# A parallel attention and FFN block: a tile of x loaded ahead, the layer norm's root taken off ScalarE, statistics held back, FFN steps moved up

## The chip, the cores and the metric

One core of a Trainium2 chip. The metric is the device time of one execution in microseconds (us), the median over several runs. The engines go by short names: PE is TensorE (matmuls), DVE VectorE, ACT ScalarE. PSUM is where the matmuls leave their results; a buffer there must be read out before it is used again.

## The reference, cut to what matters

S = 2048 rows, D = 512 columns, F = 1792, H = 32 heads of 16. The inputs are bf16.

```python
xn = _layernorm(x)                       # (x - mean) / sqrt(var + 1e-5), per row
# attention without softmax
q, k, v = split(xn @ wqkv)               # D -> 3 D
phi = lambda t: where(t > 0, t + 1, exp(t)) + 1e-6
kv  = einsum("bhsd,bhse->bhde", phi(k), v);  z = sum over s of phi(k)
o   = (phi(q) @ kv) / (phi(q) . z + 1e-6)
# the FFN, on the same xn
f   = (silu(xn @ w_gate) * (xn @ w_up)) @ w_down
out = x + o @ wo + f
```

`kv` and `z` need every row of k and v, so the attention can't begin before all 16 tiles of 128 rows are through the layer norm and the k and v projections. The FFN of a block of 512 rows needs only that block's `xn`, so its matmuls serve as filling.

## The kernel before: the parts that matter

Loads, all from one queue, in this order (block b of x is 512 rows, 512 KB):

```python
    for b in range(NB):                                   # 4 blocks
        nc.sync.dma_start(out=xb[:], in_=x2d[b * TB : (b + 1) * TB, :]...)
        if b == 0:
            nc.sync.dma_start(out=wqkv_sb[:], in_=A_wqkv...)   # 1.5 MB, q, k and v columns
    nc.sync.dma_start(out=wg_sb[:], in_=B_w_gate...)      # 1.75 MB
    nc.sync.dma_start(out=wu_sb[:], in_=B_w_up...)        # 1.75 MB
    # ... wo, w_down
```

Statistics of a block: for four tiles, then the reciprocal of a square root, improved by one Newton step:

```python
    def ln_stats_block(bb):
        for tt in range(TPB):                             # 4 tiles
            nc.vector.bn_stats(out=stats[:], in_=xbb[:, tt, :])
            nc.vector.bn_aggr(out=mv_blk[:, tt, :], in_=stats[:])
        nc.scalar.activation(out=std_blk[:], in_=mv_blk[:, :, 1], func=ACTF.Sqrt, bias=eps_ln[:], scale=1.0)
        nc.vector.reciprocal(out=rstd_blk[:], in_=std_blk[:])
        # ... vpe, and a Newton step of three operations
```

The loop. What a tile passes through, and on which engine:

```python
    stats_blk[0] = ln_stats_block(0)
    for b in range(NB):
        for tt in range(TPB):
            if tt == 1 and b + 1 < NB:
                stats_blk[b + 1] = ln_stats_block(b + 1)
            nc.vector.tensor_scalar(out=xn[:], ...)                # DVE
            # 4 transposes xn -> tp (PSUM)                         # PE
            nc.scalar.copy(out=xnT[...], in_=tp[:])                # ACT
            # 4 matmuls k_ps, 4 matmuls v_ps; both share 2 PSUM buffers ("mm")
            nc.scalar.activation(out=ek[:], in_=k_ps[:], func=ACTF.Exp)   # ACT
            # ek = min(ek, 1) + eps; pk_all = max(k_ps + 1, ek)    # DVE, frees k_ps
            nc.scalar.copy(out=v_aug[...], in_=v_ps[:]...)         # ACT, frees v_ps
            if b >= 1:
                ffn_issue(1 if b < 3 else 2, max_block=b - 1)      # low priority
        for g in range(NG):
            # 4 matmuls q_ps; eq = Exp on ACT; pqT on DVE
            ...
```

The program gives the order of priority; a scheduler makes each engine's order of it, and FFN steps have low priority, so their matmuls land where others would wait.

## Time and profile before

| | before |
|---|---|
| median, us | 241.65 (240.89 to 241.94, 16 runs) |
| profiled span, us | 239.9 |
| TensorE (PE) busy | 222.4 (93%) |
| mean granted clock | 0.993 |
| first transpose / first k matmul, us | 8.92 / 10.21 |
| loads of tables on ScalarE (ACT) | 8 |

The kernel is bound by PE, except in its first 25 us. From the view of PE's waits of the kernel before, these lines matter here, by the line that waits and the one that it waits for; the columns at the end are us in total, how often, and the longest. Left out are 2.1 us before x has landed and two short waits of 0.3 and 0.2:

```profile
PE tp L259 <- DVE xn L249: 6.5, 1, 6.5
PE k_ps L266 <- ACT xnT L260: 2.3, 2, 2.0
...
PE v_ps L266 <- DVE pk_all L283: 1.0, 2, 0.5
PE k_ps L266 <- ACT v_aug L291: 0.4, 2, 0.2
```

The first line is the start, the second the pause at 16 to 18 us which a swap of tables on ACT makes, the last two are PSUM buffers that come free late.

### The profile page before, as it was taken

The page shows a single profiled execution, that of the slowest core. Times are in us where ns is not written, and L with a number is a line of the kernel's source. Part 1 is how long each engine was busy: PE and PEld are TensorE (multiplying, and loading weights), DVE is VectorE, ACT ScalarE, POOL GpSimd, SP SyncE. Part 2 cuts the span into 40 slices and gives each one's busy share as a digit, 9 for nine tenths or more (in the row PEclk, how much of TensorE's full clock was granted, in tenths as well). Part 3 has the DMA queues.
Part 4 walks back from the last instruction along what each step waited for, and adds up shares of the span by engine and source line. Part 5 has one row for each costly group of instructions (what it writes and reads, how often), then busy time and mean ns, then how long its engine had stood idle before and what let it go on. Part 6 is the DMA issues. An engine that isn't in the chain of part 4 may idle for free.

```text
span 239.9 us, 3281 instructions
## 1 busy us (share of the span) xinstructions
PE 222.4 (93%) x1226; PEld 107.2 (45%) x1250; DVE 140.8 (59%) x324; ACT 120.6 (50%) x204; POOL 1.4 (1%) x9
## 2 busy tenths in 40 slices
PE   0469999999999999999999999999999999999994
PEld 0224455444444465444445544444554444454441
DVE  3898697686595799652129765212986521386121
ACT  2489997666656647764006566500566640056000
POOL 2000000000000000000000000000000000000000
PEclk9997999999999999999999999999999999999999
DMA  6999700000000000000000000000000000100001
GB/s 245 364 405 379 229 0 0 1 3 0 0 0 0 3 0 4 0 0 0 25 22 23 3 22 0 0 22 25 22 23 3 0 0 22 44 25 0 23 25 44
DMA packets 8352, 12.01 MB, mean 50 GB/s; under 512 B 400, under 2 KB 6800, under 8 KB 8336
## 3 DMA queue, kind: packets, MB, share of 16 engines
q1 hardware_dynamic: 8336, 11.80, 13.9%
q8 instruction: 10, 0.16, 0.3%
q14 instruction: 6, 0.05, 0.1%
HBM read 9.70 MB, written 2.10 MB: 49 GB/s over the span
## 4 chain that ended last, share of the span: by engine, by line
PE 85%; DVE 6%; ACT 6%; DMA 1%; issue 1%
PE o_ps L213 20%; PE g_ps L176 19%; PE u_ps L176 19%; PE o_ps L205 6%; PE v_ps L266 5%; PE k_ps L266 5%; PE q_ps L302 5%; PE otp L388 2%; ACT xnT L260 2%; PE num_ps L363 2%; DMA xb<-in_A_x_dram 1%; DVE stats L144 1%; PE tp L259 1%; DVE pqT L319 1%; ACT eq L310 1%
## 5 line engine op out<-in xcount | busy, mean ns | idle before, releaser
L186 ACT ACTIVATE uh<-u_ps 128x512 bf16<-128x512 f32 x56 | 33.7, 603 | 53.9 <-DVE hTf L197 42.5
L176 PE MATMUL g_ps<-xnT,wg_sb 128*128 128x512 bf16 x214 | 59.0, 380 | 0.7 <-issue 0.2
L176 PE MATMUL u_ps<-xnT,wu_sb 128*128 128x512 bf16 x219 | 58.5, 379 | 0.2
L213 PE MATMUL o_ps<-wd_sb,hTf 128*128 128x512 bf16 x219 | 51.2, 379 | 0.3
L188 DVE SCALAR_TENSOR_TENSOR wst<-th,g_ps 128x512 bf16<-128x512 bf16 x56 | 38.1, 681 | 20.0 <-ACT th L184 19.9
L184 ACT ACTIVATE th<-g_ps 128x512 bf16<-128x512 f32 x56 | 33.7, 602 | 17.7 <-PE g_ps L176 17.4
L221 DVE TENSOR_TENSOR o_t<-o_ps,xb 128x512 bf16<-128x512 f32 x16 | 11.1, 691 | 50.9 <-PE o_ps L213 50.8
L213 PEld LDWEIGHTS <-hTf 128*128 128x128 bf16 x224 | 21.5, 98 | 24.6
L176 PEld LDWEIGHTS <-wu_sb 128*128 128x128 bf16 x224 | 21.6, 98 | 23.9 <-issue 0.4
L176 PEld LDWEIGHTS <-wg_sb 128*128 128x128 bf16 x224 | 21.3, 99 | 22.1 <-issue 0.6
L197 DVE TENSOR_TENSOR hTf<-wst,uh 128x512 bf16<-128x512 bf16 x56 | 23.3, 421 | 5.9 <-ACT uh L186 5.7
L266 PEld LDWEIGHTS <-xnT 128*128 128x128 bf16 x128 | 12.7, 100 | 21.2 <-issue 6.2
L266 PE MATMUL k_ps<-wqkv_sb,xnT 128*128 128x512 bf16 x64 | 17.3, 394 | 2.7 <-ACT xnT L260 2.3
L266 PE MATMUL v_ps<-wqkv_sb,xnT 128*128 128x512 bf16 x63 | 17.3, 399 | 1.0 <-DVE pk_all L283 1.0
L205 PE MATMUL o_ps<-wo_sb,oT 128*128 128x512 bf16 x62 | 16.3, 379 | 0.1
L302 PE MATMUL q_ps<-xnT,wqkv_sb 128*128 128x512 bf16 x63 | 15.7, 378 | 0.1
L274 ACT ACTIVATE ek<-k_ps 128x512 f32<-128x512 f32 x16 | 9.7, 608 | 6.4 <-PE k_ps L266 5.9
L310 ACT ACTIVATE eq<-q_ps 128x512 f32<-128x512 f32 x16 | 9.8, 610 | 6.2 <-PE q_ps L302 5.1
L144 DVE BATCH_NORM_STATS2 stats<-xb 128x6 f32<-128x512 bf16 x16 | 10.5, 677 | 3.4 <-DMA xb<-in_A_x_dram 3.4
L259 PE MATMUL tp<-ident,xn 128*128 128x128 bf16 x64 | 6.1, 242 | 6.5 <-DVE xn L249 6.5
L380 DVE TENSOR_TENSOR o_sb<-num_ps,rden 128x512 bf16<-128x512 f32 x16 | 11.0, 688 | 1.9 <-PE num_ps L363 1.4
L291 ACT CAST v_aug<-v_ps 128x512 bf16<-128x512 f32 x16 | 9.6, 598 | 4.3 <-PE v_ps L266 4.0
(49 smaller groups left out, 148.2 us busy)
## 6 DMA issues: line engine op xcount, KB each, us to landing
xb<-in_A_x_dram SPq DMA_DIRECT2D x4, 512.0 KB, 8.5
out_dram<-o_t SPq DMA_DIRECT2D x16, 128.0 KB, 1.7
wg_sb<-in_B_w_gate_dram SPq DMA_DIRECT2D x1, 1792.0 KB, 12.6
wu_sb<-in_B_w_up_dram SPq DMA_DIRECT2D x1, 1792.0 KB, 15.6
wd_sb<-in_B_w_down_dram SPq DMA_DIRECT2D x1, 1792.0 KB, 19.4
wqkv_sb<-in_A_wqkv_dram SPq DMA_DIRECT2D x1, 1536.0 KB, 7.1
wo_sb<-in_A_wo_dram SPq DMA_DIRECT2D x1, 512.0 KB, 15.7
```

What stands on the lines that cost most here:

```text
L144: nc.vector.bn_stats(out=stats[:], in_=xbb[:, tt, :])
L176: nc.tensor.matmul(dst[:], lhsT=w_sb[:, c, f * P : (f + 1) * P], rhs=xnT[:, c, b * TB : (b + 1) * TB], start=(c == 0), stop=(c == DC - 1),)
L184: nc.scalar.activation(out=th[:], in_=g_ps[:], func=ACTF.Tanh, scale=0.5)
L186: nc.scalar.activation(out=uh[:], in_=u_ps[:], func=ACTF.Copy, scale=0.5)
L188: nc.vector.scalar_tensor_tensor(out=wst[:], in0=th[:], scalar=1.0, in1=g_ps[:], op0=ALU.add, op1=ALU.mult,)
L197: nc.vector.tensor_tensor(out=hTf[:], in0=wst[:], in1=uh[:], op=ALU.mult)
L205: nc.tensor.matmul(o_ps[:], lhsT=oT[:, c, t * P : (t + 1) * P], rhs=wo_sb[:, c, :], start=(c == 0), stop=False,)
L213: nc.tensor.matmul(o_ps[:], lhsT=hT_tiles[(b, f)][:, tt * P : (tt + 1) * P], rhs=wd_sb[:, f, :], start=False, stop=(f == FC - 1),)
L221: nc.vector.tensor_tensor(out=o_t[:], in0=o_ps[:], in1=xb_tiles[b][:, tt, :], op=ALU.add)
L266: nc.tensor.matmul(dst[:], lhsT=xnT[:, c, t * P : (t + 1) * P], rhs=wqkv_sb[:, c, (j + 1) * D : (j + 2) * D], start=(c == 0), stop=(c == D ...
L302: nc.tensor.matmul(q_ps[:], lhsT=wqkv_sb[:, c, g * P : (g + 1) * P], rhs=xnT[:, c, b * TB : (b + 1) * TB], start=(c == 0), stop=(c == DC - 1),
L310: nc.scalar.activation(out=eq[:], in_=q_ps[:], func=ACTF.Exp)
```

## The change

Its intent: begin the matmuls earlier, and take the swaps of tables out of the way of the first blocks. Four parts:

1. *Loads.* The first tile of x (128 KB) alone, then the other three; the k and v columns of `wqkv` in two halves of rows, then the q columns; the first 512 columns of `w_gate` and `w_up` right after block 1 of x, the rest after all of x.
2. *Root.* The first tile's statistics by themselves; 1/sqrt from the bits (a constant minus half the bits) and two Newton steps, nine small operations on VectorE (DVE), no `Sqrt` on ACT.
3. *Gates.* The statistics of tiles 1 to 3 are issued only after a copy that follows the first `xn`; those of block b + 1 only after block 0's third `xn`, and after block b's tiles in program order.
4. *FFN.* Two FFN steps of a block may follow directly on its q.

```diff
         xb = res.tile([P, TPB, D], BF16, name=f"xb{b}")
+        if b == 0:
+            nc.sync.dma_start(out=xb[:, 0, :], in_=x2d[0:P, :])
+            nc.sync.dma_start(out=xb[:, 1:TPB, :], in_=x2d[P:TB, :]...)
+            for half in range(2):                       # k and v columns
+                nc.sync.dma_start(out=wqkv_sb[:, 2 * half : 2 * half + 2, D:QKV], ...)
+            nc.sync.dma_start(out=wqkv_sb[:, :, 0:D], ...)
         ...
+        if b == 1:
+            FA = 512
+            for dst, src in ((wg_sb, B_w_gate), (wu_sb, B_w_up)):
+                nc.sync.dma_start(out=dst[:, :, 0:FA], in_=src[:, 0:FA]...)
+    for dst, src in ((wg_sb, B_w_gate), (wu_sb, B_w_up)):
+        nc.sync.dma_start(out=dst[:, :, FA:F], in_=src[:, FA:F]...)
 ...
-        nc.scalar.activation(out=std_blk[:], in_=mv_blk[:, :, 1], func=ACTF.Sqrt, ...)
-        nc.vector.reciprocal(out=rstd_blk[:], in_=std_blk[:])
-        # one Newton step
+        # ve = var + eps; ih = bits(ve) >> 1; bits(rstd) = 1597463007 - ih
+        for _ in range(2):
+            # Newton step: three operations on DVE
 ...
-    stats_blk[0] = ln_stats_block(0)
+    stats_blk[0] = ln_stats_block(0, 0, 1)
 ...
-            if tt == 1 and b + 1 < NB:
-                stats_blk[b + 1] = ln_stats_block(b + 1)
+            if b == 0 and tt == 1:
+                with tc.issue_after(hm_copy.ins):
+                    ln_stats_block(0, 1, TPB, tiles=stats_blk[0])
 ...
+            if b == 0 and tt == 2:
+                xn_gate = xn_ins
 ...
+        if b + 1 < NB:
+            with tc.issue_after(xn_gate.ins):
+                stats_blk[b + 1] = ln_stats_block(b + 1)
 ...  # q
+        ffn_issue(2, max_block=b)
```

More of the change, by code (lines that the diff above doesn't have):

```diff
@@ L12 @@
 F32 = mybir.dt.float32
+I32 = mybir.dt.int32
 @with_exitstack
@@ L73 @@
         xb = res.tile([P, TPB, D], BF16, name=f"xb{b}")
+        if b == 0:
+            nc.sync.dma_start(out=xb[:, 0, :], in_=x2d[0:P, :])
+            nc.sync.dma_start(
+                out=xb[:, 1:TPB, :],
+                in_=x2d[P:TB, :].rearrange("(t p) d -> p t d", p=P),
+            )
+            wqkv_sb = res.tile([P, DC, QKV], BF16, name="wqkv_sb")
+            for half in range(2):
+                nc.sync.dma_start(
+                    out=wqkv_sb[:, 2 * half : 2 * half + 2, D:QKV],
+                    in_=A_wqkv[half * 2 * P : (half + 1) * 2 * P, D:QKV].rearrange(
+                        "(c p) f -> p c f", p=P
+                    ),
+                )
+            nc.sync.dma_start(
+                out=wqkv_sb[:, :, 0:D], in_=A_wqkv[:, 0:D].rearrange("(c p) f -> p c f", p=P)
+            )
+        else:
+            nc.sync.dma_start(
+                out=xb[:],
+                in_=x2d[b * TB : (b + 1) * TB, :].rearrange("(t p) d -> p t d", p=P),
+            )
+        xb_tiles.append(xb)
+        if b == 1:
+            FA = 512
+            wg_sb = res.tile([P, DC, F], BF16, name="wg_sb")
+            wu_sb = res.tile([P, DC, F], BF16, name="wu_sb")
+            for dst, src in ((wg_sb, B_w_gate), (wu_sb, B_w_up)):
+                nc.sync.dma_start(
+                    out=dst[:, :, 0:FA], in_=src[:, 0:FA].rearrange("(c p) f -> p c f", p=P)
+                )
+    for dst, src in ((wg_sb, B_w_gate), (wu_sb, B_w_up)):
         nc.sync.dma_start(
-            out=xb[:],
-            in_=x2d[b * TB : (b + 1) * TB, :].rearrange("(t p) d -> p t d", p=P),
-        )
-        xb_tiles.append(xb)
-        if b == 0:
-            wqkv_sb = res.tile([P, DC, QKV], BF16, name="wqkv_sb")
-            nc.sync.dma_start(
-                out=wqkv_sb[:], in_=A_wqkv.rearrange("(c p) f -> p c f", p=P)
-            )
-    wg_sb = res.tile([P, DC, F], BF16, name="wg_sb")
-    nc.sync.dma_start(out=wg_sb[:], in_=B_w_gate.rearrange("(c p) f -> p c f", p=P))
-    wu_sb = res.tile([P, DC, F], BF16, name="wu_sb")
-    nc.sync.dma_start(out=wu_sb[:], in_=B_w_up.rearrange("(c p) f -> p c f", p=P))
+            out=dst[:, :, FA:F], in_=src[:, FA:F].rearrange("(c p) f -> p c f", p=P)
+        )
     wo_sb = res.tile([P, DC, D], BF16, name="wo_sb")
@@ L126 @@
     nc.tensor.matmul(hm_ps[:], lhsT=e8[:], rhs=ident[:HG, :HG], start=True, stop=True)
-    nc.vector.tensor_copy(out=hm8[:], in_=hm_ps[:])
+    hm_copy = nc.vector.tensor_copy(out=hm8[:], in_=hm_ps[:])
     xnT = res.tile([P, DC, S], BF16, name="xnT")
@@ L137, with ln_stats_block @@
     nc.vector.memset(v_aug[:, :, :, P : P + 1], 1.0)
-    def ln_stats_block(bb):
+    def ln_stats_block(bb, t0=0, t1=TPB, tiles=None):
         xbb = xb_tiles[bb]
-        mv_blk = pb.tile([P, TPB, nc.vector.BN_AGGR_DIM], F32, name="mv_blk")
-        for tt in range(TPB):
+        if tiles is None:
+            mv_blk = pb.tile([P, TPB, nc.vector.BN_AGGR_DIM], F32, name="mv_blk")
+            rstd_blk = pb.tile([P, TPB], F32, name="rstd_blk")
+        else:
+            mv_blk, rstd_blk = tiles
+        n = t1 - t0
+        for tt in range(t0, t1):
             stats = pb.tile([P, nc.vector.BN_STATS_DIM], F32, name="stats")
@@ L145, in ln_stats_block @@
             nc.vector.bn_aggr(out=mv_blk[:, tt, :], in_=stats[:])
-        std_blk = pb.tile([P, TPB], F32, name="std_blk")
-        nc.scalar.activation(
-            out=std_blk[:], in_=mv_blk[:, :, 1], func=ACTF.Sqrt, bias=eps_ln[:], scale=1.0
-        )
-        rstd_blk = pb.tile([P, TPB], F32, name="rstd_blk")
-        nc.vector.reciprocal(out=rstd_blk[:], in_=std_blk[:])
-        vpe = pb.tile([P, TPB], F32, name="vpe")
+        ve = pb.tile([P, TPB], F32, name="ve")
+        nc.vector.tensor_scalar(
+            out=ve[:, t0:t1], in0=mv_blk[:, t0:t1, 1], scalar1=EPS_LN, scalar2=None, op0=ALU.add
+        )
+        ih = pb.tile([P, TPB], I32, name="ih")
         nc.vector.tensor_scalar(
-            out=vpe[:], in0=mv_blk[:, :, 1], scalar1=EPS_LN, scalar2=-0.5, op0=ALU.add, op1=ALU.mult
+            out=ih[:, t0:t1], in0=ve[:, t0:t1].bitcast(I32), scalar1=1, scalar2=None,
+            op0=ALU.logical_shift_right,
+        )
+        nc.vector.tensor_scalar(
+            out=rstd_blk[:, t0:t1].bitcast(I32), in0=ih[:, t0:t1], scalar1=-1.0, scalar2=1597463007.0,
+            op0=ALU.mult, op1=ALU.add,
         )
         nrt = pb.tile([P, TPB], F32, name="nrt")
-        nc.vector.tensor_tensor(out=nrt[:], in0=rstd_blk[:], in1=rstd_blk[:], op=ALU.mult)
-        nc.vector.tensor_tensor(out=nrt[:], in0=nrt[:], in1=vpe[:], op=ALU.mult)
-        nc.vector.scalar_tensor_tensor(
-            out=rstd_blk[:],
-            in0=nrt[:],
-            scalar=1.5,
-            in1=rstd_blk[:],
-            op0=ALU.add,
-            op1=ALU.mult,
-        )
+        for _ in range(2):
+            nc.vector.tensor_tensor(out=nrt[:, t0:t1], in0=rstd_blk[:, t0:t1], in1=rstd_blk[:, t0:t1], op=ALU.mult)
+            nc.vector.scalar_tensor_tensor(
+                out=nrt[:, t0:t1], in0=nrt[:, t0:t1], scalar=-0.5, in1=ve[:, t0:t1], op0=ALU.mult, op1=ALU.mult
+            )
+            nc.vector.scalar_tensor_tensor(
+                out=rstd_blk[:, t0:t1], in0=nrt[:, t0:t1], scalar=1.5, in1=rstd_blk[:, t0:t1],
+                op0=ALU.add, op1=ALU.mult,
+            )
         return mv_blk, rstd_blk
@@ L248 @@
             xn = pb.tile([P, D], BF16, name="xn")
-            nc.vector.tensor_scalar(
+            xn_ins = nc.vector.tensor_scalar(
                 out=xn[:],
```

## The prediction

> **What bounds the kernel now.** I read the page's busy shares first, then its slices.
>
> ```profile
> PE 222.4 (93%) x1226; PEld 107.2 (45%) x1250; DVE 140.8 (59%) x324; ACT 120.6 (50%) x204; POOL 1.4 (1%) x9
> ...
> PE   0469999999999999999999999999999999999994
> ...
> PEclk9997999999999999999999999999999999999999
> ```
>
> TensorE (PE) is busy from slice 4 on and slack only in slices 1 to 3 and the last: the kernel is TensorE-bound except in its first 25 us or so. The second line to read is the granted clock: slice 4 (18 to 24 us) falls to 0.7. The chain of waits confirms it: 85% of the span lies on PE.
>
> How much time is loose? Steady matmuls of 512 columns start 0.216 us apart (the chain view has 14 of L213 in 3.02 us). Transposes and other 128-column matmuls start about 0.056 apart. The program has 928 of the first kind (200.3 us), 256 of the second (14.3 us) and 64 tiny ones (1.6 us): 216.2 us of work. The first transpose starts at 8.92 and the last matmul ends at 236.5, 227.6 us later. So some 11.4 us are lost between them, 8.9 before them, and 3.4 after. By the same count of what was issued, 8.92 to 28.5 (where the first q matmuls start) holds 12.1 us of work in 19.6: 7.5 us lost. From 28.5 on only about 4 to 5 us are lost in small pieces. The timeline of the first 30 us shows why:
>
> ```profile
> 4.31 1.29 DVE L144 BATCH_NORM_STATS2 stats<-xb 128x6 f32<-128x512 bf16 x2 [3.08 <-DMA xb<-in_A_x_dram]
> ...
> 8.92 1.03 PE L259 MATMUL tp<-ident,xn 128*128 128x128 bf16 x8 [6.52 <-DVE xn L249]
> ...
> 10.21 1.89 PE L266 MATMUL k_ps<-wqkv_sb,xnT 128*128 128x512 bf16 x4 [0.25 <-ACT xnT L260]
> ...
> 13.82 1.28 ACT L147 ACT_TABLE_LOAD   x1
> ...
> 15.12 0.30 ACT L147 ACTIVATE std_blk<-mv_blk,eps_ln 128x4 f32<-128x4 f32 x1
> ...
> 15.43 1.28 ACT L274 ACT_TABLE_LOAD   x1
> ...
> 16.73 0.60 ACT L274 ACTIVATE ek<-k_ps 128x512 f32<-128x512 f32 x1
> ...
> 18.34 1.04 PE L266 MATMUL k_ps<-wqkv_sb,xnT 128*128 128x512 bf16 x4 [2.03 <-ACT xnT L260]
> ```
>
> The reader is to see: x arrives at 4.3; statistics of all four tiles, then the square root, stand before the first transpose; ScalarE (ACT) swaps tables around each square root; and one such swap (13.82 to 16.73) delays `ek`, `v_aug` and then `xnT`, so that PE stands 2.03 us. The stretches of 2 us show what that pause then did to the clock:
>
> ```profile
> 18.00:20.00 2.00, 1.66 (x6) 0.67 (x7) 2.00 (x5) 1.98 (x3) 0.00 (x0) 0.81 1.03 405
> 20.00:22.00 2.00, 1.99 (x11) 1.31 (x11) 1.21 (x5) 1.96 (x4) 0.00 (x0) 0.50 1.04 383
> 22.00:24.00 2.00, 1.79 (x7) 0.76 (x7) 1.97 (x12) 1.98 (x5) 0.00 (x0) 0.83 1.09 350
> ```
>
> The column before the last two is the clock. (1-0.81)x2 + (1-0.5)x2 + (1-0.83)x2 = 1.7 us of matmul time gone.
>
> **What the Trainium skill says.** (1) "TensorE: Matmul & The Clock Gate", Part 1: the array starts at half clock, matmuls start N/1.2 ns apart cold and N/2.4 + 2.5 warm, and an idle window of about 3.4 us sends it back to half. The trace agrees: the first k matmuls at 10.21 start about 0.42 apart, later ones 0.216; the half-clock stretch lasts about 3.4 us and comes after the pause. That window was not wholly idle here. (2) "ScalarE: Activation LUTs", What ACT_TABLE_LOAD costs: 1283 ns plus about 1380 of drain; Table sets: exp and tanh share a set, sqrt does not. The load agrees (1.28); the drain does not show: from the load at 15.43 to `ek` at 16.73 is 1.30. (3) "VectorE: DVE Perf Modes", The DRAIN you can't avoid: chained operations pay a flush each, so their count is the cost. In the trace the small dependent operations of the root take 0.16 and start about 0.19 apart. (4) "DMA: Bandwidth & Descriptors", Anatomy of one DMA: about 2.0 us fixed plus bytes over 436 GB/s, fitted on another issue path. For the 512 KB of x that is 3.2; the trace has 3.48.
>
> **The change, part by part.**
>
> *First tile of x alone.* DMA over the first 5 us, in slices of 0.125 us:
>
> ```profile
> GB/s 0 0 0 0 0 0 0 0 0 0 0 0 0 0 0 98 82 90 131 156 360 385 369 393 385 393 393 410 377 451 434 369 393 418 418 393 442 393 442 393
> ```
>
> Adding up, 131 KB have moved at about 2.67 us and 524 KB at 3.68; the latter is landed at 4.28, 0.6 later. So tile 0 should be there at 2.67 + 0.6 = 3.27. The k and v columns (1 MB in two halves) end at about 7.0, at 0.39 MB per us, and are needed from 7.65 on.
>
> *Statistics of one tile, root by bits on DVE.* Before: 4 stats, a square root on ACT, 8.45 `xn`: 4.1 us from landing. After: one stats (0.70), its aggregate and 9 dependent operations at 0.19 each (1.9): `xn` at about 5.9, transposes at 6.36. Adding the old distance of 1.29 from transpose to k, k starts at 7.65 instead of 10.21: **2.6 us gained**. The bit root costs 5 chains x 9 small operations instead of 4 x 6, 45 against 24; alone some 0.08 to 0.19 each, 2 to 4 us more of DVE, in a stretch where DVE was full (10 to 20 us).
>
> *Tables.* The built order has one table load instead of eight; 7 x 1.28 + 4 x 0.30 = 10 us leave ACT, all of it before 27 us.
>
> *The walk through block 0.* Using the built order and start distances of the old trace (stats 0.60, `xn` and the min of `ek` 0.33, `pk_all` 0.60; ACT 0.5 to 0.6 each), I find: v0 cold to 11.1; k1 at 12.45 (waits for `xnT` behind `v_aug`); k2 at 15.0; k3 at 17.6; q0 at 20.2; q3 issued by 25.45. By then PE has issued 62 large matmuls and 16 transposes. Before, at 33.9, it had issued 67 and 48; without these extra 5 x 0.216 + 32 x 0.056 = 2.9 us it would stand at 31.0. **The gain at this point is 5.5 us**: 2.6 from the start, 2.9 from the pause, its half clock and the small waits. Walking on into block 1, third k tile at 32.3 against 41.63 less 3.5 of extra work, I get 5.8.
>
> *Two FFN steps after q.* They only move PE work; the count is the same. They can fill the 0.48 us hole at 86.4 between `num_ps` and `den_ps`, and some of the 0.6 at 213 to 217, where the old order had few FFN steps left. Perhaps 0.5 in all.
>
> *Sum.* 5.8 + 0.5 = 6.3. A walk by hand lets everything start the moment it can; I take 12% off: 5.5 us. 241.65 - 5.5 = **236.1 us**.
>
> **Rivals.** (a) *DVE becomes the bound of the start.* For it: DVE is busy 10.0 of 10 us from 10 to 20 us in the old trace, and the change adds 21 small operations; statistics of blocks 1 and 2 stand in its queue ahead of `pk_all`, whose end frees a PSUM buffer. Against it: the gates push these statistics behind `xn`, and DVE starts a microsecond earlier. If it wins, only the start is kept, and the time is about 238.5. (b) *The clock falls again.* Tile by tile PE now waits about a microsecond before k1 and k2; a window with too little matmul work costs another 1.7 us, giving 237.8. In the old trace a window about 40% busy fell back, one about 75% busy did not; mine are about 75%. (c) *The first 10 us are bound by the weights.* If the halves land after 8 us instead of 7.0, k0 stalls, and 1 us of the gain goes: 237. (d) *Everything fits better, and late holes close too*: 234.5.
>
> **Range and chances.** The mechanism is plain, the amount is not: the threshold of 2% lies at 236.8, only 0.7 above my number. (a) in part or (b) or (c) puts it over. I give 234.4 to 238.3, and 0.64 for faster by over 2%, 0.35 for within, 0.01 for slower: PE's work is unchanged, and no part lengthens its late stages.
>
> **What would show it.** Right: first stats at 3.2 to 3.4; first transpose at 6.2 to 6.6; k at 7.5 to 7.9; one table load; no PE wait of over 1.3 us after the first k; clock 1.0 from about 13 us on; q0 near 20 to 21 and q3 done by 26; the later stages shifted as a block by 5 to 6 us. Wrong: DVE without idle time from 6 to 27 us and PE waiting for `pk_all` or `xn`; a second half-clock stretch; k waiting for a DMA; or holes among the attention tiles, because FFN steps used early are missing there.

## The result, and the profile after

| | before | after |
|---|---|---|
| median, us | 241.65 | 236.69 (236.2 to 237.64, 8 runs) |
| ratio | 1 | 0.9798, 95% 0.9785 to 0.9812 |
| profiled span, us | 239.9 | 235.4 |
| PE busy, us | 222.4 | 221.9 |
| mean granted clock | 0.993 | 0.998 |
| first transpose / first k, us | 8.92 / 10.21 | 6.08 / 7.37 |

4.96 us less, inside the predicted range. That the kernel is faster is plain; whether by over 2%, to which the prediction gave a chance of 0.64, stays open, since the interval holds 0.98. These lines of the page of the kernel after answer to those that the prediction begins with:

```profile
PE 221.9 (94%) x1226; PEld 106.8 (45%) x1250; DVE 140.6 (60%) x349; ACT 110.9 (47%) x193; POOL 1.4 (1%) x9
...
PE   0789999999999999999999999999999999999994
...
PEclk9999999999999999999999999999999999999999
```

PE is full from the fourth slice of 6 us on, and the clock has no dip. ACT lost 11 operations and 9.7 us, DVE gained 25 small operations, and its sum stayed. The timeline of the first 26 us (start, duration, engine, line, operation; in brackets the idle time before it and what ended it):

```profile
2.93 0.69 DVE L172 BATCH_NORM_STATS2 stats<-xb 128x6 f32<-128x512 bf16 x1 [1.69 <-DMA xb<-in_A_x_dram]
...
6.08 0.61 PE L291 MATMUL tp<-ident,xn 128*128 128x128 bf16 x4 [3.68 <-DVE xn L281]
...
7.37 1.04 PE L298 MATMUL k_ps<-wqkv_sb,xnT 128*128 128x512 bf16 x2 [0.68 <-ACT xnT L292]
...
9.23 1.01 PE L298 MATMUL k_ps<-wqkv_sb,xnT 128*128 128x512 bf16 x2 [0.83 <-DMA wqkv_sb<-in_A_wqkv_dram]
...
10.19 0.41 DVE L281 TENSOR_SCALAR xn<-xb,mv_blk,rstd_blk 128x512 bf16<-128x512 bf16 x1
...
13.12 1.04 PE L298 MATMUL k_ps<-wqkv_sb,xnT 128*128 128x512 bf16 x4 [0.44 <-ACT xnT L292]
...
20.87 1.89 PE L340 MATMUL q_ps<-xnT,wqkv_sb 128*128 128x512 bf16 x8
```

x lands for the first tile at 2.93 and the first k matmul starts at 7.37. Its third and fourth chunks, however, wait for the second half of the weights until 9.23. The pause of two microseconds before the third tile's k is gone. The waits of PE, as above for the kernel before:

```profile
PE tp L291 <- DVE xn L281: 3.7, 1, 3.7
...
PE k_ps L298 <- DMA wqkv_sb<-in_A_wqkv_dram: 0.8, 1, 0.8
PE k_ps L298 <- ACT v_aug L323: 0.5, 1, 0.5
```

**Where the time came from, by equal work.** The two kernels order PE's work differently, so equal moments can't be compared tile by tile. I therefore add up PE's work in the order of each trace, 0.216 us for a matmul of 512 columns and 0.056 for a smaller one, and ask at what moment each kernel has started the same sum. The difference is the lead over the kernel before. Of the 1250 matmuls, 24 have no record in each of these two traces (the page's x1226 against x1250 weight loads; the second profile of the change has them all); I placed them by their weight loads, which are all recorded. The leads are read by straight lines between starts; read from the starts themselves they differ by up to 0.3. Counts that stand in some of the expectations below were made without this and are up to a microsecond lower.

| work started, us | 0.35 | 2 | 4 | 6 | 8 | 10 | 14 | 30 | 50 | 214 |
|---|---|---|---|---|---|---|---|---|---|---|
| moment in the kernel before | 9.4 | 12.8 | 15.7 | 20.9 | 23.7 | 26.4 | 30.3 | 47.4 | 68.1 | 232.0 |
| lead of after | 2.0 | 1.1 | 1.1 | 3.3 | 4.4 | 5.1 | 4.9 | 4.9 | 4.6 | 4.5 |
| lead of its second profile | 1.9 | 1.5 | 1.5 | 3.7 | 4.8 | 5.5 | 5.3 | 5.3 | 4.9 | 4.9 |

The lead at the first k matmul is 2.84. By equal work it falls to 1.1. About 1 us of that is the wait for weights: with the k columns loaded first, an experiment below that takes this wait away, it stays at 2.1. The rest is order, since the kernel before transposes two tiles ahead of its first k, and the change one. The lead then rises by 4.0 where the kernel before has its pause and its half clock (from 15.7 to 26.4 us there), and then stays, less some 0.4 to 0.6. The profiled run took 237.16 us, 0.5 more than the median; its lead of 4.5 at the end is that run's.

### The profile page after: what moved, and what is told of

Same layout as the page of the kernel before. It is cut to its first block, busy times and chain, and to the rows that moved or that the text cites. A ratio compares the mean times of both kernels' runs of the same rounds, so it can differ in the third digit from the quotient of the medians.

```text
span 235.4 us, 3299 instructions
## 1 busy us (share of the span) xinstructions
PE 221.9 (94%) x1226; PEld 106.8 (45%) x1250; DVE 140.6 (60%) x349; ACT 110.9 (47%) x193; POOL 1.4 (1%) x9
## 4 chain that ended last, share of the span: by engine, by line
PE 85%; DVE 7%; DMA 3%; ACT 2%; issue 1%; SPq 1%; ACTq 0%
PE o_ps L244 20%; PE g_ps L207 20%; PE u_ps L207 19%; PE o_ps L236 6%; PE k_ps L298 5%; PE v_ps L298 5%; PE q_ps L340 5%; DMA wqkv_sb<-in_A_wqkv_dram 3%; PE otp L427 2%; PE num_ps L402 2%; PE kvz_ps L370 1%; DVE xn L281 1%; DVE hTf L228 1%; DVE pqT L357 1%; ACT uh L217 1%
## 5 line engine op out<-in xcount | busy, mean ns | idle before, releaser
L207 PE MATMUL u_ps<-xnT,wu_sb 128*128 128x512 bf16 x219 | 59.1, 379 | 0.3
L244 PE MATMUL o_ps<-wd_sb,hTf 128*128 128x512 bf16 x220 | 52.1, 379 | 0.3
L215 ACT ACTIVATE th<-g_ps 128x512 bf16<-128x512 f32 x56 | 33.4, 597 | 18.0 <-PE g_ps L207 17.8
L228 DVE TENSOR_TENSOR hTf<-wst,uh 128x512 bf16<-128x512 bf16 x56 | 22.6, 422 | 10.8 <-PE o_ps L244 7.9
L298 PEld LDWEIGHTS <-xnT 128*128 128x128 bf16 x128 | 12.4, 99 | 19.3 <-issue 5.7
L340 PE MATMUL q_ps<-xnT,wqkv_sb 128*128 128x512 bf16 x62 | 15.8, 378 | 0.4 <-ACT v_aug L323 0.2
L315 DVE SCALAR_TENSOR_TENSOR pk_all<-k_ps,ek 128x512 bf16<-128x512 f32 x16 | 10.9, 683 | 0.3
```

What stands on the lines that cost most here:

```text
L207: nc.tensor.matmul(dst[:], lhsT=w_sb[:, c, f * P : (f + 1) * P], rhs=xnT[:, c, b * TB : (b + 1) * TB], start=(c == 0), stop=(c == DC - 1),)
L215: nc.scalar.activation(out=th[:], in_=g_ps[:], func=ACTF.Tanh, scale=0.5)
L228: nc.vector.tensor_tensor(out=hTf[:], in0=wst[:], in1=uh[:], op=ALU.mult)
L244: nc.tensor.matmul(o_ps[:], lhsT=hT_tiles[(b, f)][:, tt * P : (tt + 1) * P], rhs=wd_sb[:, f, :], start=False, stop=(f == FC - 1),)
L298: nc.tensor.matmul(dst[:], lhsT=xnT[:, c, t * P : (t + 1) * P], rhs=wqkv_sb[:, c, (j + 1) * D : (j + 2) * D], start=(c == 0), stop=(c == D ...
L315: nc.vector.scalar_tensor_tensor(out=pk_all[:, t, :], in0=k_ps[:], scalar=1.0 + EPS_PHI, in1=ek[:], op0=ALU.add, op1=ALU.max,)
```

## The experiments

Theory: the time comes from the start (loads, first tile's statistics) and from the swaps of tables that no longer stand before `xnT`. The rivals give each part to something else: to the FFN steps, to the order that the gates make on DVE, or have a removed wait come back as another. In the expectations theories and rivals go by letters, explained where each first comes; k0, k1, v1 are the k and v matmuls of the first and second tile. Twelve runs, in three groups; the kernel before had medians of 241.58, 241.66 and 241.72 us in them.

### The root alone

On the kernel before, only part 2, for a whole block at a time:

```diff
-        nc.scalar.activation(out=std_blk[:], ..., func=ACTF.Sqrt, ...)
+        # ve, bits >> 1, magic - bits, two Newton steps (DVE)
```

> The kernel before with one edit: the square root by bits on DVE in place of Sqrt on ACT (one table load instead of eight); loads, statistics of four tiles at once and FFN order stay. Theory P (the pause of 2.0 us behind the table swaps and the half clock after it are worth about 2.4 us of their own): 239.2 us (238.7 to 239.8), first k matmul still at 10.2 to 10.6, no PE wait over 1.3 us after it, clock 1.0 from about 13 us on. Rival S (only the earlier start counts; the pause is slack that later work would have met anyway): 241.2 or more.

Measured: 240.29 us (239.43 to 240.5, 4 runs), ratio 0.9946 (0.9916 to 0.9975). The timeline of PE:

```profile
9.39 1.18 PE L264 MATMUL tp<-ident,xn 128*128 128x128 bf16 x8 [6.98 <-DVE xn L254]
10.67 1.89 PE L271 MATMUL k_ps<-wqkv_sb,xnT 128*128 128x512 bf16 x4
...
17.40 1.02 PE L271 MATMUL k_ps<-wqkv_sb,xnT 128*128 128x512 bf16 x4 [0.67 <-ACT v_aug L296]
```

The pause of 2.03 us has become one of 0.67, there is one load of tables, and no second stretch of half clock. The lead goes from -0.8 at 2 us of work to +2.35 at 10: about 3 us are regained where they should be. But the first transpose is 0.47 later than before (the nine dependent operations against a root on ACT), and 1.8 is left in this profile, 1.3 in the medians. So the pause does cost what was put down for it, but the root alone keeps only 1.3 us of that, which lies between theory P and rival S.

### The change with Sqrt back

```diff
-        # ve, bits >> 1, magic - bits, two Newton steps (DVE)
+        nc.scalar.activation(out=std_blk[:, t0:t1], ..., func=ACTF.Sqrt, ...)
+        # reciprocal, one Newton step
```

> The changed kernel with Sqrt on ACT put back, one tile first as before it: eight table loads again; loads and FFN steps as changed. Theory P: the start is kept (first k at 7.2 to 7.8), the swaps come back into block 0 and 1: 238.9 us (238.2 to 239.7). Rival S: 236.7 to 237.2.

Measured: 240.18 us (239.92 to 240.59, 4 runs), ratio 0.9949 (0.993 to 0.9969). The timeline, of ACT and PE:

```profile
15.80 1.28 ACT L175 ACT_TABLE_LOAD   x1
...
24.32 1.02 PE L336 MATMUL q_ps<-xnT,wqkv_sb 128*128 128x512 bf16 x4 [1.30 <-ACT v_aug L319]
...
30.78 0.39 PE L287 MATMUL tp<-ident,xn 128*128 128x128 bf16 x4 [1.43 <-ACT xnT L288]
```

The start is even better (first transpose 5.43, because the table of `Sqrt` is loaded anyway at 0.8 us and its chain is shorter), and the lead reaches 5.25 at 10 us of work. Then the swaps, of which the first line shows one, take some of it: 3.8 at 12, 2.1 at 20, 1.8 at the end. The swaps cost 3.5 us here, more than I had put down for them (238.9 us expected). The two halves are not additive: the root alone brings 1.3 us, everything but the root 1.4, both together 5.0.

### The change without the early FFN steps

```diff
-        ffn_issue(2, max_block=b)
```

> The changed kernel without the two FFN steps after each block's q. Theory (they only move work, since the two traces lose the same 5.0 us in the later stages): 236.7 us (236.3 to 237.1). Rival F (they fill q's waits for eq and pqT, and the holes at the start of attention): 237.6 or more.

Measured: 236.94 us (236.25 to 237.7, 4 runs), ratio 0.9814 (0.9787 to 0.9842), against 0.9798 for the change. The two steps are worth nothing that these runs can tell. Its lead also shrinks between 30 and 50 us of work (6.1 to 5.7), as that of the change does, and is flat from there.

### The k columns first

The wait of k for the second half of the weights, taken away by other loads: k columns whole, then v columns.

```diff
-            for half in range(2):      # rows, k and v columns
+            for part in (1, 2):        # k columns, then v columns
```

> The changed kernel with the k columns of wqkv loaded whole first and the v columns after them, instead of two halves of k and v rows. k0 of the changed kernel stood 1.25 us for the second half, which landed at 9.2. Theory W (that wait is on the path until the second tile's xn at 10.2 takes over, so most of it comes back): k0 runs through from 7.4, 235.8 us (235.4 to 236.3). Rival D (DVE's root for tiles 1 to 3 and xn at 10.2 bound this stage anyhow): 236.5 to 236.8.

Measured: 236.61 us (236.52 to 236.72, 4 runs), ratio 0.98 (0.9784 to 0.9816). The timeline of PE:

```profile
7.37 1.89 PE L296 MATMUL k_ps<-wqkv_sb,xnT 128*128 128x512 bf16 x4 [0.68 <-ACT xnT L290]
9.05 1.92 PE L296 MATMUL v_ps<-wqkv_sb,xnT 128*128 128x512 bf16 x4
...
18.35 1.02 PE L296 MATMUL v_ps<-wqkv_sb,xnT 128*128 128x512 bf16 x4 [0.24 <-DVE pk_all L313]
...
23.35 1.02 PE L338 MATMUL q_ps<-xnT,wqkv_sb 128*128 128x512 bf16 x4 [0.31 <-DVE pqT L355]
```

k runs through, v starts at 9.05 instead of 10.04, and the wait is gone; the time isn't lower, as rival D had it. Against the second profile of the change the lead is 0.6 higher at 4 us of work (2.1 to 1.5) and equal at the end (4.9): small waits for DVE (`pk_all`, `pqT`) take it back. One caution: the weights' wait is not the same in all runs. With the loads of the change it was 0.8 us in one profile, 0.4 in the second and 0.6 with `Sqrt` back, and the profiles of two others with the same first loads (without the early FFN steps, and without the early gate and up slices) had none. In all five the second half landed late, between 8.2 and 9.2 us; k needs it at 8.2. So the change's median probably holds only part of the wait.

### The loads back

The change, with the loads of the kernel before:

```diff
-    # tile 0 alone; k/v halves, q; gate and up in two parts
+    # x blocks whole, wqkv whole, gate and up whole after x
```

> The changed kernel with the loads of the kernel before (four whole x blocks, wqkv in one piece, gate and up whole); one tile's statistics first, bits, gates and FFN steps as changed. x then lands at 4.3, not 2.9, but wqkv is there at 8.4 without a late half. Theory L (the early tile counts, because the second tile's xn, behind DVE, sets the stage): first transpose 7.4, xn of the second tile at 11.5 against 10.2, 237.8 us (237.3 to 238.3). Rival M (the split is worth nothing, since k0 then stood for its weights until 9.2 anyway): 236.5 to 237.0.

Measured: 238.79 us (238.68 to 239.31, 4 runs), ratio 0.9888 (0.9874 to 0.9902). First transpose 7.45, first k 8.74: 1.37 later than with the change's loads. The lead is 3.9 at 10 us of work and 2.7 at the end. The loads are worth 2.1 us in all, more than their head start, and a microsecond more than expected; the run with gate and up whole, below, looks into that.

### The root on ACT for block 0 only

With k columns first, as above: `Sqrt` and one Newton step for block 0, whose table is there anyway; bits for blocks 1 to 3.

```diff
+        if bb == 0:
+            nc.scalar.activation(out=std[:, t0:t1], ..., func=ACTF.Sqrt, ...)
+            nc.vector.reciprocal(...)
+        else:
             # bits
-        for _ in range(2):
+        for _ in range(1 if bb == 0 else 2):
```

> k columns first, and Sqrt on ACT for block 0 alone (the first table load is then for sqrt, one more for exp behind the second Sqrt), bits for blocks 1 to 3. With all roots on ACT the first transpose stood at 5.43 against 6.08, since the chain on DVE is shorter, and the lead over the kernel before was 4.6 us after 10 us of PE work, lost again to the swaps of blocks 1 to 3. Theory H (DVE's chain of nine small operations costs 0.65 at the start and as much for tiles 1 to 3; leaving it out there pays): k1 at 11.5 against 12.1, 236.0 us (235.6 to 236.3). Rival D (later waits for pk_all and v_aug take it back): 236.5 to 236.9.

Measured: 236.66 us (236.49 to 238.26, 5 runs), ratio 0.9808 (0.9783 to 0.9832). The timeline, of PE and DVE:

```profile
5.44 0.61 PE L296 MATMUL tp<-ident,xn 128*128 128x128 bf16 x4 [3.05 <-DVE xn L286]
...
11.17 0.69 DVE L170 BATCH_NORM_STATS2 stats<-xb 128x6 f32<-128x512 bf16 x1 [1.22 <-DMA xb<-in_A_x_dram]
...
13.50 1.02 PE L303 MATMUL v_ps<-wqkv_sb,xnT 128*128 128x512 bf16 x4 [1.00 <-DVE pk_all L320]
```

A start 0.64 us earlier, and no gain: DVE now comes so early to the statistics of block 1 that their x isn't there, stands 1.22 us, and behind that stands `pk_all`, for which PE waits 1.00. A removed wait came back as another. One of the five runs took 238.26 us at a mean clock of 0.991, so the clock may have fallen in it; it was not profiled.

### One Newton step

With k columns first: bits for all blocks, one step instead of two (three operations less in the first chain).

```diff
-        for _ in range(2):
+        for _ in range(1):
```

> k columns first and one Newton step instead of two in every chain (the result is less exact, it may miss the tolerance). Takes three dependent operations of 0.19 out of each chain: first transpose at 5.5, 15 small DVE operations fewer. Theory H: 236.1 us (235.7 to 236.4). Rival D: 236.5 to 236.9.

Measured: 236.56 us (236.4 to 237.43, 4 runs), ratio 0.9799 (0.9781 to 0.9817); the result is still within the reference's tolerance. The first transpose moves up by some 0.6 us, and the time stays, as in the run before.

### No gates

```diff
-                with tc.issue_after(hm_copy.ins):
-                    ln_stats_block(0, 1, TPB, tiles=stats_blk[0])
+                ln_stats_block(0, 1, TPB, tiles=stats_blk[0])
 ...
-            with tc.issue_after(xn_gate.ins):
-                stats_blk[b + 1] = ln_stats_block(b + 1)
+            stats_blk[b + 1] = ln_stats_block(b + 1)
```

> The changed kernel without its two gates on when statistics are issued. In the built order three more stats then stand ahead of the first xn. Theory G (the order on DVE matters at the start): first transpose at about 7.2 or later, 237.4 us (237.0 to 238.2). Rival (xn of tiles 1 and 2 come early in exchange, so nothing is lost): 236.5 to 236.9.

Measured: 238.16 us (237.93 to 238.42, 4 runs), ratio 0.9858 (0.9843 to 0.9873). The timeline of PE:

```profile
7.62 0.61 PE L290 MATMUL tp<-ident,xn 128*128 128x128 bf16 x4 [5.22 <-DVE xn L280]
9.91 0.58 PE L290 MATMUL tp<-ident,xn 128*128 128x128 bf16 x4 [1.68 <-DVE hm L149]
10.29 1.91 PE L297 MATMUL k_ps<-wqkv_sb,xnT 128*128 128x512 bf16 x4
```

Without gates the first k is where it was in the kernel before (10.29 against 10.21), although x comes as early as in the change: the other tiles' statistics stand before the first `xn` and before the copies that PE's second group of transposes waits for. The gates are worth 1.5 us, half of the early start.

### The change once more

> The changed kernel once more, unaltered, as the measure for the three beside it: 236.7 us (236.2 to 237.2).

Measured: 236.85 us (236.44 to 236.94, 4 runs), ratio 0.9794 (0.9782 to 0.9807). The result holds. The third row of the table of leads is from this profile.

### Block 1's statistics behind the first `pk_all`

The kernel with `Sqrt` for block 0, with the gate moved to the operation that was delayed there:

```diff
-            if b == 0 and tt == 2:
-                xn_gate = xn_ins
+            if b == 0 and tt == 0:
+                xn_gate = pk_ins
```

> As the version with Sqrt on ACT for block 0, but block 1's statistics are held until the first pk_all is issued. In that version these statistics, waiting 1.22 us for the second x block, stood on DVE ahead of the first ek and pk_all, and v of the second tile waited 1.0 us. Theory Q (that queueing on DVE is what ate the earlier start): no such wait, v1 at about 12.3 against 13.5, 235.6 us (235.2 to 236.1). Rival (the stage is bound by its own chain of small waits, whatever the order): 236.4 to 236.8.

Measured: 236.21 us (235.72 to 236.65, 4 runs), ratio 0.9771 (0.9758 to 0.9783). The timeline of PE:

```profile
11.64 1.31 PE L303 MATMUL k_ps<-wqkv_sb,xnT 128*128 128x512 bf16 x4 [0.31 <-ACT xnT L297]
12.79 1.03 PE L303 MATMUL v_ps<-wqkv_sb,xnT 128*128 128x512 bf16 x4
```

The second tile's v starts at 12.79 instead of 13.50 without a wait for `pk_all`, and the lead at 10 us of work is 6.2, at the end 5.4. It is the fastest version, some 0.6 us below the change in the same rounds; the two intervals (to 0.9783, from 0.9782) just touch, so the order is likely and not proven. The time lies between what theory Q (up to 236.1) and its rival (from 236.4) had expected. The wait is gone as Q had it, but of the 0.7 us at the second tile's v only 0.3 is left at the end (a lead of 5.4 against 5.1 with the gate where it was), since q now waits 0.5 us for `pqT`. It supports, and doesn't prove, that the order on DVE decides what an earlier start is worth.

### Gate and up weights whole

The change, with `w_gate` and `w_up` in one load each, after x:

```diff
-            for dst, src in ((wg_sb, B_w_gate), (wu_sb, B_w_up)):
-                nc.sync.dma_start(out=dst[:, :, 0:FA], ...)
```

> The changed kernel with gate and up loaded whole again, after all of x; x and wqkv split as changed. With all loads put back the time was 238.8 where 237.8 was expected. Theory U (the early slices of gate and up carry the difference, since without them FFN work comes too late to fill block 0): first u matmul at about 22, 237.4 us (237.1 to 237.9). Rival (the whole 2.1 us is the early x tile): 236.5 to 236.9.

Measured: 241.3 us (239.99 to 242.8, 6 runs), ratio 0.9984 (0.9947 to 1.0022). The timeline of PE, then the stretches of 2 us (length, busy time of PE, weight load, DVE, ACT and POOL, then granted clock, DMA share, GB/s):

```profile
15.58 1.03 PE L293 MATMUL v_ps<-wqkv_sb,xnT 128*128 128x512 bf16 x4
18.64 0.46 PE L202 MATMUL g_ps<-xnT,wg_sb 128*128 128x512 bf16 x1 [2.03 <-DMA wg_sb<-in_B_w_gate_dram]
18.89 1.91 PE L293 MATMUL k_ps<-wqkv_sb,xnT 128*128 128x512 bf16 x4
```

```profile
18.00:20.00 2.00, 1.36 (x4) 0.57 (x5) 0.90 (x3) 0.00 (x0) 0.00 (x0) 0.71 1.03 404
20.00:22.00 2.00, 2.00 (x6) 0.73 (x5) 0.53 (x4) 0.60 (x1) 0.00 (x0) 0.50 1.01 401
```

Nearly the whole gain is gone, much more than I had expected. The gate's matmuls stand in PE's order before the fourth tile's k, and PE keeps its order: it waits 2.03 us for weights that the load now brings later. And that pause sends the clock to half from 18.8 to 22.3 us, just as the old one did. The lead falls from 4.0 at 6 us of work to 1.6 at 8 and 0.55 at the end. The runs fall into groups: two at about 240.0, with a mean clock of 1.0, and four at 241.3 to 242.8, with 0.993; so a fall of the clock goes with 1.3 us or more here. What parts the four, two at 241.3 and two above 242.6, is not known. In the run with all loads back the same whole loads cost less. There the gate's weights land at 17.36 instead of 18.59, and the first gate matmul comes at 17.8 without a wait; that its start, 1.4 us later, makes the difference is argued from the two timelines, not shown.

### More PSUM buffers for k, v and q

The fastest version, with three "mm" buffers and three "gu" (for the gate's and up's matmuls) instead of two and four:

```diff
-    MM_BUFS = 2
-    GU_BUFS = 4
+    MM_BUFS = 3
+    GU_BUFS = 3
```

> As the version with the later gate, with three PSUM buffers for mm and three for gu in place of two and four. In block 0 of the changed kernel k2 and k3 wait 0.6 us each for v_aug to free their buffer. Theory B (these waits are on the path): 0.6 to 1.2 us faster than the version beside it, 234.8 us. Rival (three gu buffers hold up FFN in the 200 us after, where the kernel has no slack): 237 or more.

Measured: 236.32 us (235.94 to 236.64, 4 runs), ratio 0.9775 (0.9763 to 0.9788): the same as with two, so neither theory B (234.8) nor its rival (237 or more) held. PE's waits after its first transpose, in the fastest version and then in this run:

```profile
PE k_ps L303 <- ACT xnT L297: 1.0, 2, 0.7
PE q_ps L345 <- DVE pqT L362: 0.5, 1, 0.5
PE k_ps L303 <- ACT v_aug L328: 0.5, 1, 0.5
```

```profile
PE k_ps L303 <- ACT xnT L297: 2.4, 4, 0.9
```

The third buffer does take the waits for `v_aug` and `pqT` away, but those for `xnT` grow from 1.0 us to 2.4. Again a removed wait came back as another. Two things changed in this run; that one gu buffer less costs nothing is thus likely, not shown.

## Why the prediction was right, and where it was off

The time (236.1 predicted, 236.69 measured) and the mechanism held. Step by step, for the walk through block 0, from the profile of the change:

| step | predicted, us | measured, us |
|---|---|---|
| first tile of x there | 3.27 | 2.93 |
| first transpose | 6.36 | 6.08 |
| first k | 7.65 | 7.37 |
| second half of k and v columns there | 7.0 | 9.2 |
| second tile's k | 12.45 | 13.12 |
| third, fourth tile's k | 15.0, 17.6 | 15.69, 18.28 |
| first q | 20.2 | 20.87 |
| last q issued by | 25.45 | 25.81 |

- **The start** was right: 2.6 us predicted, 2.84 measured at the first k. (The 3.2 us that it gives for a load of 512 KB is an estimate from the skill's figures; the walk itself rests on the trace.) The early loads and the gates are both needed for it (first k at 8.74 and 10.29 without the one or the other).
- **The pause, its half clock and the small waits** were about right in their sum, 2.9 us predicted. From 2 to 14 us of work, where block 0's last q is issued, the lead grows by 3.8 in the change, by 3.2 with the k columns first, where no wait for weights has to be made good, and by 2.9 with the root alone. The clock stays full from 12.4 us on. In the rival (b) a window of little work was to bring the half clock back. The windows of the change were 74% busy at the lowest (12.4 to 15.8 us), as estimated, and it didn't. With gate and up whole, a window 40% busy did bring it. The prediction's window "about 75% busy" of the old trace was 81% (2.77 of the 3.41 us from 12.43), so its comparison was looser than it looked.
- **The half clock's own share**, 1.7 us in the prediction, is the part of that sum that the runs don't bear out. The kernel before ran now with and now without it: 11 of its runs beside the experiments had a mean clock of 0.99 and took 241.64 us on the mean, the 16 at 0.998 to 1.0 took 241.61. So the gain of this stage is better put down to the pause and the waits around it. A likely reason, which no run tests: in that stretch ACT was busy 1.98, 1.96 and 1.98 of each 2 us (the lines in the prediction), so a faster PE would have waited for ACT. With gate and up whole, where the half clock does go with 1.3 us, ACT was busy 0.00 and 0.60.
- **The weights** were the term that was off in the walk: their second half landed at 9.2 in this profile, not at 7.0. This is rival (c). The late landing stands in every profile with these loads (8.2 to 9.2); only the wait comes and goes. From 5.0 to 6.5 us the DMA moved 217, 152 and 254 GB/s in half microseconds, where the estimate had taken 390 throughout, and where the kernel before moved 381, 412 and 338. But the 1 us that rival (c) would have cost isn't found in the time: with the k columns first, the wait is gone and the median 0.1 to 0.2 lower. What probably stands between is rival (a) in part: `xn` of the second tile comes at 10.19 because DVE works through three tiles' statistics first, and later `pk_all` and `pqT` hold the buffers. Four experiments (k first, `Sqrt` in block 0, one Newton step, the moved gate) put the start 0.6 to 1 us ahead; only the one that also changed DVE's order kept a part of it.
- **The gain at the last q**: 5.5 us predicted, 4.9 by equal work in this profile and 5.3 in the second. Two slips make up most of the difference in this profile: counted over all weight loads, the kernel before starts the same 62 large and 16 small matmuls at 30.6, not 31.0, and the change is done with its last q 0.36 later than in the walk.
- **The root's operations on DVE** were miscounted: the kernel before has 5 to a block, 20 and not 24, so 25 came on top and not 21. The 2 to 4 us more of DVE did not show (140.8 busy before, 140.6 after).
- **After that** the prediction failed, by a small term: 0.3 us more in block 1 and 0.5 us for filled holes late. Neither is left at the end. The lead shrinks by 0.4 from there on, and without the two FFN steps it does the same. The hole at 86.4 was indeed closed: `den_ps` waits 0.3 us for DVE in the kernel before, not at all in the change, and there the lead rises by 0.4, only to lose it again within 10 us of work. But the run without the two steps shows the same, so it wasn't they that closed it. What took the 0.4 is not settled.
- **The discount** of 12% on the sum (6.3 to 5.5 us) stood for such things, and was slightly too small: 4.96 came. That the total came so near is in part luck: the half clock and the late terms were counted and not found, and the waits around the pause gave more than they were counted for.
- **Not seen at all** was the weight of the early gate and up slices. The prediction counted them as no gain, since before nothing waited for these weights. In the change's PE order they hold 4.4 us (241.3 against 236.85 in the same rounds), because block 0's FFN matmuls moved forward to fill PE's waits. That the change had these slices in it was, for the prediction, luck.

So the parts don't add up because each opens what the next one closes. The start without the root meets the swaps; the root without the start has a longer chain; both without the early slices run into the weights, and into the half clock again.

## What to carry to other kernels

Price a removed wait by what is next behind it: ask which engine's queue decides when the tile after this one starts, since here a head start of 0.6 us did not show in the time, and with the queue on DVE in another order some half a microsecond came of it (likely, not proven). When work is moved forward, move its loads forward with it, and check over several runs whether a stretch of half clock shows in the time: here it went with 1.3 us or more in one kernel and with nothing in another. Measure parts by taking each away from the whole, and also by adding it alone, for the two can differ threefold.

## What the Trainium skill lacked or had wrong

- "TensorE: Matmul & The Clock Gate", Part 1, gives an idle window of about 3.4 us as what sends the clock back to half; its passage on short idle times between groups of matmuls tells of a clock that falls without one, but gives no share. Here the windows before the fall weren't idle: PE was busy for 41% of the 3.41 us before 19.25 us in the kernel before, and for 40% before 18.83 us with gate and up whole. Windows 74% busy (the change, from 12.41), 62% and 57% (`Sqrt` back, from 21.55 and 28.38) and 51% (`Sqrt` for block 0, from 10.02) kept the clock full. These windows are counted in steps of 3.41 us from the moment at which the clock rose, since in the kernel before its changes, at 12.43, 19.25 and 22.66, lie such steps apart. The limit, somewhere between 41% and 51% by these profiles, was not measured.
- "ScalarE: Activation LUTs", What ACT_TABLE_LOAD costs, adds about 1.38 us of drain to a load. None was seen: from the start of a load at 15.43 us to the next operation at 16.73 are 1.30 us, the load itself being 1.28.
- No page tells of what was met with several small loads in the queue at the start: for 1.5 us the DMA of the change fell from about 370 to between 152 and 254 GB/s. Every profile with split loads has such a dip, by different amounts (90 to 287 GB/s in its lowest half microsecond), and none of the three with the kernel before's few large loads has one (338 or more). Its cause is open.
